# A decode step with cached attention: loops for the query and key products, one product for the maximum, x added by VectorE, the last values in four pieces, branch hints at the ends of two programs

## The chip, the cores and the metric

The kernel runs on one core of one Trainium2 chip. It is written for the engines directly, without a scheduler: TensorE (PE) multiplies, VectorE (DVE) does element work, reductions and transposes, ScalarE (ACT) exponentials and GELU, GpSimd (POOL) a few small passes, and SyncE (SP) issues nearly all DMA transfers. The metric is device time in microseconds (us), the median of three runs.

## The reference

One token passes through an attention block with a cache and then through an MLP block. All inputs are bfloat16.

```python
h  = x + A(layernorm(x))          # x: 1 x 1 x 512
h2 = h + B(layernorm(h))
# A: 32 query heads, 8 key heads, 16384 cached positions, head size 128
q = (x @ wq) ...                  # wq: 512 x 4096
scores = q . k * 128 ** -0.5
p = softmax(scores)
o = p . v
A = o @ wo                        # wo: 4096 x 512
# B, for one position: its shifted parts are all zeros, so x1 = x
h2 = gelu(layernorm(x1) @ w3) @ w4      # w3: 512 x 1792, w4: 1792 x 512
B = x1 + h2
```

Four query heads share a key head. With a sequence of length one the four shifted slices of the MLP's first stage hold only padding, so w1 and w2 do not enter the result, and the kernel never loads them. What it must read is wq (4 MB), keys and values (32 MB each), wo (4 MB), w3 and w4 (1.8 MB each).

## The kernel before

The work goes by pairs of key heads: four pairs, each with 8 MB of keys and 8 MB of values. Three big buffers in SBUF hold what is loaded: `kb[0]` and `kb[1]` (4 MB each, the two halves y = 0 and 1 of a pair's keys) and `vb` (8 MB, a pair's values). wq comes into `vb` first, wo into `kb[0]` and w3 and w4 into `kb[1]` at the end. SP issues the loads in program order, each when the last readers of its buffer are done: `load_keys(j + 1, y)` (L361) waits for the key transposes of half y, `load_values(j + 1)` (L370) for the value products of pair j. The keys of pair 1 come as one load of 8 MB, the other keys as two of 4 MB.

`Program` (L24) collects operations per engine with what they read and write, works out the semaphore waits and writes out each engine's program. SP, ACT, POOL and DVE get straight programs (`_run`, L128). TensorE's program has a loop over the pairs (`_tensor`, L136): block `pe_pair` with an inner block `pe_half` run twice (L206) and then `pe_rest` (L220); registers hold the semaphore values to wait for. Behind the loop stands a branch that is never taken, `pe_leave` (L236), which carries a branch hint marked at the start of the program (L191).

The stages:

- Start: x is loaded as 4 rows, spread over the partitions by a product with `quarter` (L463), and normalised on DVE (`row_sums` L392, `variance`, `seeds`, `inverse_root`), giving `xn`.
- Query product (L497 to L504): 32 products of 64 columns by 512, written out, four per half row of a PSUM bank; eight DVE transposes (L505) and four copies (L511) bring the query into `qb`.
- Per pair: DVE copies the pair's query to `qn` (L592). Per half: eight key transposes of 128x1024 words (L520), each followed on TensorE by four score products (L528) that add into one PSUM bank; the products are written out, 32 per half.
- `softmax` (L536): a maximum per row on DVE (L539), a product that turns it into a row (L540), a maximum per head on DVE (L542), a product that spreads it over the partitions (L544), the bias (L546), the exponential on ACT (L550), two transposes (L554).
- `values` (L557): 64 products of 32 columns by 512 (L562) when the whole 8 MB of values have landed.
- `gather` (L567): the sum of the exponentials by a product (L570), four DVE passes (L575, L578), a product (L581), the reciprocal (L583), the result into `o_m` (L584).
- Tail: 32 products with wo (L624), a product that adds x (L628), a copy (L631), four products (L633), the second normalisation, w3 (L645), GELU on ACT (L657), transposes (L661), w4 (L666), the last sum (L670) and the store (L672).

## Time and profile before

| what | us |
|---|---|
| median of 3 runs | 191.99 |
| lowest, highest | 191.99, 193.09 |
| profiled execution, its own time | 192.09 |
| its span, from the first to the last instruction | 190.8 |
| TensorE products busy | 109.7 |
| VectorE busy | 116.7 |
| ScalarE busy | 9.1 |
| GpSimd busy | 7.4 |

The span is taken by the hardware profiler inside the execution; 1.3 us of the execution's own time lie around it. The profile page gives busy times per engine, a row that shows the mean busy share of the 16 DMA engines in 40 equal slices, the DMA queues, and the chain of work that ended last. Lines of the timeline read: start, duration, engine, line, operation, output and inputs, and in brackets the idle time ahead of it and what ended it. Queue issues of SP are marked SPq. The clock that TensorE was granted was 0.82 in the mean, with stretches at 0.5. Memory reads come to 79.17 MB, at a mean of 415 GB/s over the span.

### The profile page before, as it was taken

The page shows a single profiled execution, that of the slowest core. Times are in us where ns is not written, and L with a number is a line of the kernel's source. Part 1 is how long each engine was busy: PE and PEld are TensorE (multiplying, and loading weights), DVE is VectorE, ACT ScalarE, POOL GpSimd, SP SyncE. Part 2 cuts the span into 40 slices and gives each one's busy share as a digit, 9 for nine tenths or more (in the row PEclk, how much of TensorE's full clock was granted, in tenths as well). Part 3 has the DMA queues.
Part 4 walks back from the last instruction along what each step waited for, and adds up shares of the span by engine and source line. Part 5 has one row for each costly group of instructions (what it writes and reads, how often), then busy time and mean ns, then how long its engine had stood idle before and what let it go on. Part 6 is the DMA issues. An engine that isn't in the chain of part 4 may idle for free.

```text
span 190.8 us, 1799 instructions
## 1 busy us (share of the span) xinstructions
PE 109.7 (58%) x694; PEld 41.3 (22%) x694; DVE 116.7 (61%) x184; ACT 9.1 (5%) x15; POOL 7.4 (4%) x16
## 2 busy tenths in 40 slices
PE   0128099892093006999256599934749896056543
PEld 0113034220031002432013133211313322022213
DVE  7746497984404009998443999935289995503372
ACT  3000000002000000000200000010000000500020
POOL 7100000000000000000000000000000000000041
PEclk9999958999559755899958879995797999558975
DMA  6999999999999999997999999979999899999990
GB/s 227 433 440 440 440 440 441 440 440 440 440 440 440 440 440 440 440 426 344 433 440 440 543 440 426 440 337 440 426 426 488 371 440 398 440 423 411 433 371 20
DMA packets 2612, 79.22 MB, mean 415 GB/s; under 512 B 304, under 2 KB 432, under 8 KB 560
## 3 DMA queue, kind: packets, MB, share of 16 engines
q1 hardware_dynamic: 2600, 79.17, 96.7%
q8 instruction: 2, 0.03, 0.1%
q14 instruction: 2, 0.02, 0.0%
q10 hardware_dynamic: 8, 0.00, 0.0%
HBM read 79.17 MB, written 0.00 MB: 415 GB/s over the span
## 4 chain that ended last, share of the span: by engine, by line
DMA 60%; DVE 32%; PE 5%; issue 1%; ACT 1%; SPq 1%; ACTq 0%
DMA kb<-in_A_k_cache_dram 45%; DVE kt L520 28%; DMA kb<-in_B_w_dram 15%; PE O_ps L562 3%; DVE pt L554 1%; PE mn_ps L666 1%; DVE mx L539 1%; ACT p_sb L550 1%; SPq L355 1%; DVE od L578 1%; PE s_ps L528 1%; PE A_ps L581 0%; PE mn_ps L544 0%; PE mn_ps L540 0%; DVE od L575 0%
## 5 line engine op out<-in xcount | busy, mean ns | idle before, releaser
L528 PE MATMUL s_ps<-kt,qn 128*128 128x512 bf16 x256 | 70.2, 417 | 26.0 <-DVE kt L520 23.9
L520 DVE STREAM_TRANSPOSE kt<-kb 128x1024 int32<-128x1024 int32 x64 | 72.8, 1208 | 15.0 <-DMA kb<-in_A_k_cache_dram 15.0
L528 PEld LDWEIGHTS s_ps<-kt,qn 128*128 128x128 bf16 x256 | 23.5, 104 | 71.9 <-issue 36.6
L562 PE MATMUL O_ps<-vb,pt 128*32 128x512 bf16 x256 | 22.6, 530 | 21.7 <-DMA vb<-in_A_v_cache_dram 13.5
L575 DVE TENSOR_SCALAR od<-O_ps,rowc 128x128 f32<-128x128 f32 x4 | 1.4, 350 | 28.3 <-PE mn_ps L570 28.3
L562 PEld LDWEIGHTS O_ps<-vb,pt 128*32 128x32 bf16 x256 | 8.5, 128 | 34.2 <-issue 23.9
L554 DVE STREAM_TRANSPOSE pt<-p_sb 64x1024 bf16<-64x1024 bf16 x8 | 9.9, 1239 | 5.4 <-ACT p_sb L550 5.3
L550 ACT ACTIVATE p_sb<-s_ps,bias 128x1024 bf16<-128x1024 f32 x4 | 4.5, 1114 | 156.0 <-DVE nmh L546 156.0
L539 DVE TENSOR_REDUCE mx<-s_ps 128x1 f32<-128x1024 f32 x4 | 4.9, 1224 | 4.6 <-PE s_ps L528 4.6
L438 POOL TENSOR_SCALAR st<-st 128x1 f32<-128x1 f32 x1 | 0.2, 242 | 177.4 <-DVE st L423 177.4
L501 PE MATMUL O_ps<-vb,xn 128*64 128x512 bf16 x16 | 3.3, 586 | 5.8 <-DMA vb<-in_A_wq_dram 5.8
L581 PE MATMUL A_ps<-od,zo 128*32 128x128 f32 x8 | 1.6, 285 | 6.4 <-DVE den L583 6.4
L540 PE MATMUL mn_ps<-ident_f,mx 128*1 128x128 f32 x8 | 1.5, 270 | 5.3 <-DVE mx L539 5.3
L578 DVE SCALAR_TENSOR_TENSOR od<-O_ps,rowc,od 128x128 f32<-128x128 f32 x12 | 4.2, 351 | 0.4
L460 DVE CAST ident<-ident_f 4x4 bf16<-4x4 f32 x1 | 3.8, 3849 | 0.6 <-POOL ident_f L455 0.6
L505 DVE STREAM_TRANSPOSE qcol<-O_ps 128x256 f32<-128x256 f32 x4 | 1.6, 428 | 4.0 <-PE O_ps L501 4.0
L463 PE MATMUL O_ps<-x,quarter 4*128 4x128 bf16 x1 | 0.3, 283 | 5.8 <-DVE quarter L461 5.8
L501 PEld LDWEIGHTS O_ps<-vb,xn 128*64 128x64 bf16 x16 | 1.5, 165 | 7.2 <-issue 7.2
L666 PE MATMUL mn_ps<-kb,hcol 128*32 128x128 bf16 x56 | 1.7, 309 | 2.0 <-DMA kb<-in_B_w_dram 2.0
L645 PE MATMUL s_ps<-kb,hc 128*32 128x448 bf16 x16 | 1.7, 572 | 1.4 <-DMA kb<-in_B_w_dram 1.4
L624 PE MATMUL O_ps<-kb,o_b 128*32 128x512 bf16 x32 | 1.9, 380 | 1.1 <-DVE o_b L620 1.1
L584 DVE SCALAR_TENSOR_TENSOR o_m<-A_ps,den,maskdd 32x128 f32<-32x128 f32 x4 | 1.4, 340 | 1.7 <-PE A_ps L581 1.7
(78 smaller groups left out, 45.0 us busy)
## 6 DMA issues: line engine op xcount, KB each, us to landing
kb<-in_A_k_cache_dram SPq DMA_DIRECT2D x6, 4096.0 KB, 23.2
vb<-in_A_wq_dram SPq DMA_DIRECT2D x1, 4096.0 KB, 12.4
kb<-in_A_wo_dram SPq DMA_DIRECT2D x1, 3072.0 KB, 27.0
kb<-in_B_w_dram SPq DMA_DIRECT2D x1, 1792.0 KB, 24.6
kb<-in_B_w_dram SPq DMA_DIRECT2D x1, 1280.0 KB, 27.9
kb<-in_A_wo_dram SPq DMA_DIRECT2D x1, 1024.0 KB, 29.1
kb<-in_B_w_dram SPq DMA_DIRECT2D x1, 384.0 KB, 28.4
kb<-in_B_w_dram SPq DMA_DIRECT2D x1, 128.0 KB, 28.2
```

The costliest lines, as they stand in the source:

```text
L355: P.op(by, lambda e: e.dma_start(dst, src), w=[key, *also], dma=name)
L460: dve(lambda e: e.tensor_copy(ident[:, :], ident_f[0:4, 0:4]), r=["ident_f"], w=["ident"])
L501: pe(lambda e, row=row, k=k, g=g, at=at: e.matmul(row[64 * g:64 * g + 64, :], copies(xn[:, k:k + 1], 64), wq_sb[:, at:at + REP * DH], star ...
L520: dve(lambda e, view=view: e.transpose(view(kt), view(kb[y])), r=[("r", y, n) for n in range(RPARTS)], w=[("kt", t)])
L528: pe(lambda e, n=n, c=c: e.matmul(s_ps[:, bass.ds(P.y, 1), :], qn[:, n, QPAD - 4 * c:QW - 4 * c], ktv[:, n // 2, n % 2, :, 8 * c:8 * c + 8 ...
L539: dve(lambda e: e.tensor_reduce(mx[:, :], s_all, AX.X, ALU.max), r=[("s", 0), ("s", 1)], w=["mx"], **both)
L550: act(lambda e: e.activation(p_sb[:, :], s_all, ACTF.Exp, bias=bias[:, 0:1], scale=float(SCALE), accum_out=acc[:, :]), r=[("s", 0), ("s", ...
L554: dve(lambda e, g=g: e.transpose(pt[64 * g:64 * g + 64, :, :, g, :], p_sb[64 * g:64 * g + 64, :]), r=["p"], w=["pt"])
L562: pe(lambda e, q=q, ct=ct, xl=xl, ch=ch: e.matmul(O_ps[0][32 * ct:32 * ct + 32, :], pt[:, xl, ch, :, :].rearrange("p g u -> p (g u)"), til ...
L578: dve(lambda e, block=block, c=c: e.scalar_tensor_tensor(od[:, :], block, rowc[:, c:c + 1], od[:, :], ALU.mult, ALU.add), r=[key, "rowc", ...
L624: pe(lambda e, r_=r_, q=q: e.matmul(O_ps[0][32 * q:32 * q + 32, :], copies(o_b[:, r_:r_ + 1], 32), wo_sb[:, r_ * D:(r_ + 1) * D], start=(r ...
L666: pe(lambda e, m=m, o=o: e.matmul(n_ps[32 * o:32 * o + 32, 0:128], hcol[:, m, :], w4_sb[:, m, o * 128:(o + 1) * 128], start=(m == 0), stop ...
```

## The change

- Query product: 32 products of the full 128 columns in a loop of eight rounds with four products each; each round writes a PSUM bank of its own, chosen by a register. Four transposes of 64 partitions by 1024 replace eight of 128 by 256.
- Key product: a loop of eight pieces per half with four products each; a register picks the slice of the query and of the transposed keys. A product with zeros now starts the bank ahead of the loop. The key transposes go two pieces at a time, except in the last half of the last pair; each adds as many to the semaphore as it holds pieces.
- Maximum: the row maxima are multiplied into a diagonal on DVE, and one product with the constant `mean4` (all entries -1 / (32 * 512)) gives every partition the negated row; DVE takes minima. The second product and its constant go.
- The sum of the exponentials and its reciprocal move ahead of the value products.
- Values: TensorE waits for a semaphore that GpSimd raises when a load has landed. The last pair's values are loaded in four pieces of 2 MB, and the value products go in four parts of 16.
- x: the spread x is kept in `hx`, and DVE adds it in the pass that also sums the row; the product at L628 goes.
- Programs: all work stands in a block named `body`; the programs of DVE and TensorE end with a branch that is never taken and carries a hint marked at their start, and the branch and hint behind the pair loop go.
- A helper `more` for extra products is added; nothing calls it.

```diff
...
+    def _vector(self):
+        eng = self.nc.vector
+        rv = eng.alloc_register("never")
+        hint = eng.mark_branch_hint_location()
+        eng.reg_mov(rv, 0)
+        self._run(eng, self.ops["DVE"], {})
+        eng.br_lt(rv, 0, "body", "pe_query").branch_hint(hint)
...
-        nc.switch_bb("pe_leave", parent=None)
-        eng.br_lt(rj, 0, "pe_pair", "pe_after").branch_hint(hint)
...
+        nc.switch_bb("pe_query", parent=None)
+        width = D
+        self.b = eng.snap(rk, min_val=0, max_val=2 * pairs - 1)
+        self.c = eng.snap(rq, min_val=0, max_val=width * (2 * pairs - 1))
+        for o in query:
+            self._issue(eng, o)
+        eng.reg_add(rk, rk, 1)
+        eng.reg_add(rq, rq, 2 * width)
+        eng.br_lt(rq, 2 * width * pairs, "pe_query", "pe_queried")
+        nc.switch_bb("pe_queried", parent=None)
+        self.b = self.c = None
+        eng.reg_add(rq, rq, width - 2 * width * pairs)
+        eng.br_lt(rq, 2 * width, "pe_query", "pe_pair")
...
+        for a in places("clear", 1, 0):
+            self._issue(eng, at[a])
+        eng.reg_mov(rq, QPAD)
+        eng.reg_mov(rk, 0)
+        eng.br("pe_piece")
+        nc.switch_bb("pe_piece", parent=None)
+        self.q = eng.snap(rq, min_val=0, max_val=QPAD)
+        self.k = eng.snap(rk, min_val=0, max_val=8 * (pieces - 1))
+        eng.reg_add(r, r, 1)
+        eng.wait_ge(vector, r)
+        for a in places("key", 1, 0, 1):
+            self._issue(eng, at[a])
+        eng.reg_add(rq, rq, -4)
+        eng.reg_add(rk, rk, 8)
+        eng.br_lt(rk, 8 * pieces, "pe_piece", "pe_halved")
...
+        straight("middle")
+        for x in range(parts):
+            eng.reg_add(rl, rl, 1)
+            eng.wait_ge(sem, rl)
+            for a in places("value", 1, x):
+                self._issue(eng, at[a])
+        straight("rest")
+        eng.reg_add(r, r, first - (final - step))
+        eng.br_lt(rl, v0 - 1 + parts * pairs, "pe_pair", "pe_after")
...
+        eng.br_lt(rl, 0, "pe_pair", "pe_end").branch_hint(hint)
+        nc.switch_bb("pe_end", parent=None)
...
-            load("v", vb[:, :], pair_rows(A_v_cache, j), "v")
+            n = 64 * DH
+            if j < PAIRS - 1:
+                load("v", vb[:, :], pair_rows(A_v_cache, j), ("v", 0),
+                     also=[("v", x) for x in range(1, 4)] + [("landed", x) for x in range(4)])
+                P.op("POOL", lambda e: e.nop(), r=[("v", 0)], w=[("landed", x) for x in range(4)], worth=4,
+                     own="v")
+                return
+            for x in range(4):
+                load(f"v{x}", vb[:, x * n:(x + 1) * n], pair_rows(A_v_cache, j)[:, x * n:(x + 1) * n], ("v", x),
+                     also=[("landed", x)])
+            for x in range(4):
+                P.op("POOL", lambda e: e.nop(), r=[("v", x)], w=[("landed", x)], own="v")
...
-            dve(lambda e: e.tensor_scalar(hr[:, :], row[:, 0:128], 0.0, 0.0, ALU.add, ALU.add,
-                                          accum_out=rs[i][:, 0:1]), r=[key], w=["hr", ("rs", i, 0)], bank=[key])
+            h, hk = (hr, "hr") if i else (hx, "hx")
+            if i:
+                dve(lambda e: e.scalar_tensor_tensor(h[:, :], row[:, 0:128], 1.0, hx[:, :], ALU.mult, ALU.add,
+                                                     accum_out=rs[i][:, 0:1]),
+                    r=[key, "hx"], w=[hk, ("rs", i, 0)], bank=[key])
...
-        rows = [(O_ps[0][:, :], ("O", 0)), (O_ps[1][:, :], ("O", 1)), (s_ps[:, 0, :], ("s", 0)), (s_ps[:, 1, :], ("s", 1))]
-        for j, (row, key) in enumerate(rows):
+        keys = [("s", 0), ("s", 1), ("O", 0), ("O", 1), "A", "mn", "spare0", "spare1"]
+        wq_k = wq_sb[:, 0:NCH * HQ * DH].rearrange("p (k c) -> p k c", k=NCH)
+        for i, key in enumerate(keys):
+            P.part("query", i)
             for k in range(NCH):
-                for g in range(2):
-                    at = k * HQ * DH + (2 * j + g) * REP * DH
-                    pe(lambda e, row=row, k=k, g=g, at=at: e.matmul(
-                        row[64 * g:64 * g + 64, :], copies(xn[:, k:k + 1], 64), wq_sb[:, at:at + REP * DH],
-                        start=(k == 0), stop=(k == NCH - 1)), r=["xn", "v"], w=[key], bank=[key])
+                pe(lambda e, k=k: e.matmul(banks[:, bass.ds(P.b, 1), :], copies(xn[:, k:k + 1], 128),
+                                           wq_k[:, k, bass.ds(P.c, REP * DH)], start=(k == 0), stop=(k == NCH - 1)),
+                   r=["xn"] + [("v", x) for x in range(4)], w=["n" if key == "mn" else key], bank=[key])
+        P.part()
+        for g in range(2):
+            row = banks[64 * g:64 * g + 64, PAIRS * g:PAIRS * g + PAIRS, :].rearrange("p j c -> p (j c)")
             for b in range(2):
-                dve(lambda e, j=j, b=b, row=row: e.transpose(
-                    qcol[:, j, 2 * REP * b:2 * REP * (b + 1), :].rearrange("p m u -> p (m u)"),
-                    row.rearrange("p (h b i e) -> p b e h i", b=2, i=32, e=2)[:, b, :, :, :]),
-                    r=[key], w=["qcol"], bank=[key])
+                dve(lambda e, g=g, b=b, row=row: e.transpose(
+                    qcol[64 * g:64 * g + 64, 2 * b:2 * b + 2, :, :].rearrange("p e m u -> p (e m u)"),
+                    row.rearrange("p (m b i e) -> p b e m i", b=2, i=32, e=2)[:, b, :, :, :]),
+                    r=["n" if x == "mn" else x for x in keys[PAIRS * g:PAIRS * g + PAIRS]], w=["qcol"],
+                    bank=keys[PAIRS * g:PAIRS * g + PAIRS])
...
-        def transpose_keys(y, ts):
-            for t in ts:
+        def transpose_keys(y, n):
+            for t in range(0, 8, n):
                 view = lambda x, t=t: x[:, :].bitcast(I32).rearrange("p (x l w) -> p x (l w)", x=2, l=64)[
-                    :, :, t * 512:(t + 1) * 512]
-                dve(lambda e, view=view: e.transpose(view(kt), view(kb[y])),
-                    r=[("r", y, n) for n in range(RPARTS)], w=[("kt", t)])
+                    :, :, t * 512:(t + n) * 512]
+                P.op("DVE", lambda e, view=view: e.transpose(view(kt), view(kb[y])),
+                     r=[("r", y, i) for i in range(RPARTS)], w=[("kt", t + i) for i in range(n)], worth=n)
         ktv = kt[:, :].rearrange("p (x l b s e) -> p b e x l s", x=2, l=64, b=2, s=32, e=2)
-        def scores(j, y, cs):
-            for c in cs:
+        none = qn[:, 0, 0:1]
+        def scores(j, y):
+            P.part("clear", j, y)
+            pe(lambda e: e.matmul(s_ps[:, bass.ds(P.y, 1), :], copies(none, 128), copies(none, 512),
+                                  start=True, stop=False, skip_group_check=True),
+               r=["qn"], w=[("s", y)], bank=[("s", y)])
+            for c in range(8):
+                P.part("key", j, y, c)
                 for n in range(4):
-                    pe(lambda e, n=n, c=c: e.matmul(
-                        s_ps[:, bass.ds(P.y, 1), :], qn[:, n, QPAD - 4 * c:QW - 4 * c],
-                        ktv[:, n // 2, n % 2, :, 8 * c:8 * c + 8, :],
-                        start=(c == 0 and n == 0), stop=(c == 7 and n == 3)),
+                    pe(lambda e, n=n: e.matmul(
+                        s_ps[:, bass.ds(P.y, 1), :], qn[:, n, bass.ds(P.q, 128)],
+                        ktv[:, n // 2, n % 2, :, bass.ds(P.k, 8), :],
+                        start=False, stop=(n == 3), skip_group_check=True),
                        r=["qn", ("kt", c)], w=[("s", y)], bank=[("s", y)])
...
-            pe(lambda e: e.matmul(m_ps[0:1, 0:128], mx[:, :], ident_f[:, :], start=True, stop=True),
-               r=["mx", "ident_f"], w=["m"], bank=["mn"])
-            dve(lambda e: e.tensor_reduce(nm[:, :, :], m_ps[0:1, 0:128].rearrange("o (g n h) -> o g h n", g=2, h=REP),
-                                          AX.X, ALU.max), r=["m"], w=["nm"], bank=["mn"])
-            pe(lambda e: e.matmul(n_ps[:, 0:2 * REP], nscale[0:1, :], nm[:, :, :].rearrange("o g h -> o (g h)"),
-                                  start=True, stop=True), r=["nm", "nscale"], w=["n"], bank=["mn"])
-            dve(lambda e: e.scalar_tensor_tensor(nmh[:, :], n_ps[:, 0:2 * REP], 1.0,
-                                                 maskgh[:, :, :].rearrange("p g h -> p (g h)"), ALU.mult, ALU.mult,
-                                                 accum_out=bias[:, :]), r=["n", "maskgh"], w=["nmh", "bias"],
-                bank=["mn"])
+            dve(lambda e: e.tensor_scalar(mxd[:, :], ident_f[:, :], mx[:, 0:1], None, ALU.mult),
+                r=["mx", "ident_f"], w=["mxd"])
+            pe(lambda e: e.matmul(m_ps[:, 0:128], mean4[:, :], mxd[:, :], start=True, stop=True),
+               r=["mxd", "mean4"], w=["m"], bank=["mn"])
+            dve(lambda e: e.tensor_reduce(nm[:, :, :], m_ps[:, 0:128].rearrange("p (g n h) -> p g h n", g=2, h=REP),
+                                          AX.X, ALU.min), r=["m"], w=["nm"], bank=["mn"])
+            dve(lambda e: e.scalar_tensor_tensor(nmh[:, :], nm[:, :, :].rearrange("p g h -> p (g h)"),
+                                                 32 * D * SCALE, maskgh[:, :, :].rearrange("p g h -> p (g h)"),
+                                                 ALU.mult, ALU.mult, accum_out=bias[:, :]),
+                r=["nm", "maskgh"], w=["nmh", "bias"])
...
         def values(j):
             tiles = vb[:, :].rearrange("p (x c l d) -> p x l c d", x=4, c=8, l=8)
-            for q in range(16):
-                for ct in range(4):
-                    xl, ch = 2 * q + ct // 2, ct % 2
-                    pe(lambda e, q=q, ct=ct, xl=xl, ch=ch: e.matmul(
-                        O_ps[0][32 * ct:32 * ct + 32, :], pt[:, xl, ch, :, :].rearrange("p g u -> p (g u)"),
-                        tiles[:, xl // 8, xl % 8, 4 * ch:4 * ch + 4, :], start=(q == 0), stop=(q == 15)),
-                       r=["v", "pt"], w=[("O", 0)], bank=[("O", 0)])
+            for x in range(4):
+                P.part("value", j, x)
+                for it in range(4):
+                    for ct in range(4):
+                        l, ch = 2 * it + ct // 2, ct % 2
+                        pe(lambda e, x=x, l=l, ct=ct, ch=ch: e.matmul(
+                            O_ps[0][32 * ct:32 * ct + 32, :], pt[:, 8 * x + l, ch, :, :].rearrange("p g u -> p (g u)"),
+                            tiles[:, x, l, 4 * ch:4 * ch + 4, :], start=(x == 0 and l < 2), stop=(x == 3 and l >= 6)),
+                           r=[("landed", x), "pt"], w=[("O", 0)], bank=[("O", 0)])
+        def sums(j):
+            pe(lambda e: e.matmul(n_ps[0:32, 32:33], zd[:, :], acc[:, :], start=True, stop=True),
+               r=["acc", "zd", "pt"], w=["n"], bank=["mn"])
+            dve(lambda e: e.reciprocal(den[:, :], n_ps[0:32, 32:33]), r=["n"], w=["den"], bank=["mn"])
         def gather(j):
...
-                transpose_keys(y, range(8))
-                scores(j, y, range(8))
+                transpose_keys(y, 1 if j == PAIRS - 1 and y else 2)
+                scores(j, y)
                 if j < PAIRS - 1:
                     load_keys(j + 1, y)
+            P.part("middle", j)
+            softmax(j)
+            sums(j)
+            values(j)
...
-        pe(lambda e: e.matmul(h_ps[:, 0:128], quarter[:, :, :].rearrange("p q u -> p (q u)"), x4[:, :],
-                              start=True, stop=False, skip_group_check=True),
-           r=["quarter", "x4"], w=[hkey], bank=[hkey])
         dve(lambda e: e.tensor_copy(osum[:, :], O_ps[0][:, :]), r=[("O", 0)], w=["osum"], bank=[("O", 0)])
         for q in range(4):
             pe(lambda e, q=q: e.matmul(h_ps[32 * q:32 * q + 32, 0:128], copies(row32[:, 0:1], 32),
-                                       osum[:, q * 128:(q + 1) * 128], start=False, stop=True, skip_group_check=True),
+                                       osum[:, q * 128:(q + 1) * 128], start=True, stop=True),
...
```

## The prediction, made before the changed kernel was run

> **What bounds the kernel now.** I read the page first: the share of the DMA engines, the queues and the chain that ended last.

> ```profile
> span 190.8 us, 1799 instructions
> ...
> DMA  6999999999999999997999999979999899999990
> ...
> q1 hardware_dynamic: 2600, 79.17, 96.7%
> q8 instruction: 2, 0.03, 0.1%
> q14 instruction: 2, 0.02, 0.0%
> ...
> DMA 60%; DVE 32%; PE 5%; issue 1%; ACT 1%; SPq 1%; ACTq 0%
> ```

> The reader sees one queue, q1, that keeps sixteen DMA engines busy for 96.7% of the span. The 32% of DVE in the chain mislead: the chain steps to DVE because a transpose released the issue of a load, but the load then stood in a full queue. The timeline of SP, the issuing engine, shows how early each load was issued:

> ```profile
> 18.40 0.33 SPq L355 DMA_DIRECT2D vb<-in_A_v_cache_dram  x1
> 42.41 0.33 SPq L355 DMA_DIRECT2D kb<-in_A_k_cache_dram  x1
> 58.55 0.33 SPq L355 DMA_DIRECT2D vb<-in_A_v_cache_dram  x1
> 81.09 9.29 SPq L355 DMA_DIRECT2D kb<-in_A_k_cache_dram  x2
> 103.26 0.33 SPq L355 DMA_DIRECT2D vb<-in_A_v_cache_dram  x1
> 115.04 9.34 SPq L355 DMA_DIRECT2D kb<-in_A_k_cache_dram  x2
> 137.30 0.33 SPq L355 DMA_DIRECT2D vb<-in_A_v_cache_dram  x1
> ```

> The trace's packet records give when the transfer ahead of each landed (sixteen 4-byte marks per transfer, one from each DMA engine; the last one counts): 32.14, 52.04, 71.39, 90.74 (and 100.45 for the second of the two issues), 110.18, 129.53 (139.25), 148.96. So the issues were early by 13.7, 9.6, 12.8, 9.6, 6.9, 14.5 and 11.7 us. An issue needs about 1.0 us (first issue 0.72, first packet 1.74). The queue never ran dry, and the tightest place is the third values, with 6.9 - 1.0 = 5.9 us. Whatever happens ahead of an issue is free up to that sum.

> The tail is the one place where time can move. Its timeline:

> ```profile
> 182.20 0.40 ACT L639 ACTIVATE hc<-hT,st 128x128 bf16<-128x128 f32 x1 [17.03 <-DVE st L404]
> ...
> 183.42 1.69 PE L645 MATMUL s_ps<-kb,hc 128*32 128x448 bf16 x16 [1.45 <-DMA kb<-in_B_w_dram]
> ...
> 185.15 0.85 ACT L657 ACTIVATE hg<-s_ps,st 128x224 bf16<-128x224 f32 x2 [2.55 <-PE s_ps L645]
> 185.67 1.04 DVE L661 STREAM_TRANSPOSE hcol<-hg 128x224 bf16<-128x224 bf16 x2 [0.83 <-ACT hg L657]
> ...
> 187.06 1.71 PE L666 MATMUL mn_ps<-kb,hcol 128*32 128x128 bf16 x56 [1.96 <-DMA kb<-in_B_w_dram]
> 188.80 0.29 DVE L670 TENSOR_TENSOR fin<-xsum,mn_ps 128x128 bf16<-128x128 f32 x1 [2.09 <-PE mn_ps L666]
> 189.12 0.63 SPq L672 DMA_DIRECT2D out_dram<-fin  x1
> ```

> Both product groups start 0.6 us after the last mark of their load: w3's at 182.81, the first part of w4's at 186.46. Those last marks are late by themselves: of w3's sixteen, fourteen are in by 181.80, the others at 182.40 and 182.81. The records say why. Four packets of the run are instructions, not data (the q8 and q14 lines above). One of 8 KB at 31.75 stretches a data packet on its engine to 3.042 us (median 2.420), and in every transfer from there on one engine ends 0.6 us behind the fifteenth (52.04 against 51.46; still 178.10 against 177.50). One of 16 KB at 180.24 stretches a packet of w3 to 1.039 (median 0.537), one at 184.72 a packet of w4 to 1.044 (0.387). The fourth, at 188.42, follows the data.

> **The change, part by part.**
> *Loops and fewer instructions.* By the order of instructions, TensorE's program shrinks from about 542 to 438 (a product counts as a weight load and a product, a float32 one twice that); DVE's from about 196 trace records to 180 (28 key transposes fewer, some others added). The two fetches put down to DVE come at its records 56 and 192, so 180 do not reach the second. TensorE fetched nothing while its pair loop ran (its hint stood right behind that loop), and the two q8 packets come after the loop ended at 176.33. With the hints at the ends of both programs I take it that no fetch falls into the data. That is the one term that counts. Bounds: all four stay as they are (0), or the three go.

> *The sum of the tail.* w3's last mark goes from 182.81 to 181.80, -1.01. The last values in 4 pieces make packets of 16 KB: between 14336 bytes at 0.537 and 24576 at 0.912 that is 0.612 each, four 2.448 against 2.420, over 8 per engine +0.22, and three more marks +0.03: +0.25. So w3's products start at 183.42 - 0.76 = 182.66; hc ends at 182.60 now and no later after, so it doesn't hold them. From there GELU and its transposes take 3.29 to 186.71, but GELU also needs the inverse root, now done at 184.84 (0.31 before GELU). hc and the root move up with the output product: the last values land in four pieces, 48 of 64 products are done before the last piece, the gather comes about 2 us earlier, but the wo products then wait for wo's own load (marks to 178.10), which leaves 0.3 to 0.8. I take -0.65 for hcol: 186.06. The first part of w4 is in on the undisturbed engines at 184.88, + 0.25 + 0.6 = 185.7, so hcol now decides: products at 186.1 instead of 187.06, -0.95. The 1.71 of products, fin and the store stay. The profiled execution took 192.09 (span 190.8 and 1.3 around it), 0.1 above the median 191.99: 192.09 - 0.95 = **191.1**.

> *Query product as a loop.* 32 full-width products against 32 of 64 columns, two of which ran side by side (16 in 3.31 us, then 16 in 1.91). Full-width rows of L528 give 0.427 and 0.213 us at half and full clock; from 13.27 at half until about 16.5, then full: 7 x 0.427 + 25 x 0.213 = 8.3 us, to 21.6 against 18.31; branches of 0.22 (below) lie beside running products. Four transposes of 64x1024 follow, two behind the products: the page has 1.24 for 64x1024 from SBUF. With the copies the first key transpose moves from 22.84 to about 26, the second half from 33.23 to about 35. First values: 13.7 of cover; keys 1: 9.6. Cost 0.

> *Key product as a loop.* Not shown by the page's busy rows, but the trace has records of such instructions in the old loops: a fused register operation 41 to 52 ns (2 or 3 steps), a compare-and-branch 79 not taken and 220 to 245 taken. A piece has seven fused operations of 2 to 6 steps; at 5 ns a step more, 0.37 us, and 0.22 for the branch, 0.1 to dispatch: 0.7 against 1.14 of a key transpose (9.13 for 8). Bounds: 0.6, and 1.3 if six steps cost twice three's. Even 1.3 adds 16 x 0.16 = 2.6 us to a pair, below 5.9. A clearing product adds 0.2 to 0.4 per half. Cost 0. Transposes in twos: between equal and 0.07 saved each; the last two pieces' eight products then trail by 1.7 instead of 0.9. In the last half the pieces are single.

> *Maximum in one product.* Out: one product with its two hops (161.76 to 162.18, 0.42); in: one DVE pass over 128x128 float32 (L398: 0.29). -0.1 per pair on a covered chain, 0. The denominator moves ahead of the values: 0.3 to 0.5 us of TensorE, covered. x on VectorE: replaces a product that ran at 179.54 beside osum; the DVE pass keeps its 0.29. 0. GpSimd passes the values' landing on: one hop, 0.05 to 0.2; in the last pair wo's load covers it.

> [...]

> **Rivals.**
> - *The fetches stay, or come elsewhere in the data* (0.2). For it: no row shows a hint on DVE at work. Then only the 16 KB pieces are left: 192.09 + 0.25 = 192.3 (191.8 to 192.8).
> - *Slower: the key loop becomes TensorE's bound* (0.12), by a fetch at its back branches or by address operations far dearer than their shorter kin. It decides from 5.9 / 16 = 0.37 us per piece above the transposes' 1.14, that is 1.51. At 2.0 a pair's chain grows by 16 x 0.86 = 13.8, the third values are 7.9 late, the next pair adds some 6: about 206; at 1.7, 9.0 - 5.9 = 3 and about as much again: 198. Against it: 0.22 per taken branch and no instruction packet from 31.75 to 180.24 in eight passes of the old half loop.
> - *The tail also runs at full clock* (0.1). L666 took 1.71 at a granted 0.5; the clock windows move with TensorE's work. Then 0.5 to 0.8 less: 190.4.

> **How the numbers follow.** My forecast has 0.58, with 190.6 to 191.8 as its own range. The range 190.2 to 192.9 takes in the first and third rivals and leaves out the slower one. A measurement here can tell about 1% (1.9 us) from no change. Faster by over 1% means below 190.1: a piece of the third rival, 0.06. Slower by over 1%, above 193.9: 0.12. Within 1%: 0.82.

> **What would show it.** Right: the q8 and q14 instruction lines of the queues vanish or fall behind the data; w3's products start near 182.7, w4's near 186.1; DMA still in nines throughout; the values' issues still earlier than the transfer ahead lands. Wrong: instruction packets inside the span, key products spaced over 1.5 us a piece, a slice of the DMA row below 7 in the middle, or an issue after the queue drained.

## The result, and the profile after

The changed kernel takes 200.61 us (median of 4 runs, 199.21 to 201.18). Against the kernel before on the same chip its ratio is 1.0426, with an interval of 1.0369 to 1.0483: it is slower, and 200.61 lies far outside the range of 190.2 to 192.9. The profiled execution took 199.21, 7.12 more than the one of before.

These are rows of the changed kernel's profile page, the same ones as were shown of before:

```profile
span 196.6 us, 2321 instructions
...
DMA  6999999999999999998999999999999999999800
...
q1 hardware_dynamic: 3032, 79.17, 94.0%
q14 instruction: 1, 0.01, 0.0%
...
DVE 35%; PE 33%; DMA 20%; issue 8%; ACT 2%; ACTq 0%; DVEq 0%; SPq 0%
```

Two things are to be seen. The DMA row holds its nines (one 8 among them) until the loads are done, and its last two slices are empty: the loads are no later than before, and something else ends last. The chain of waits says what: DMA falls from 60% to 20%, PE rises from 5% to 33%. And one instruction packet is left inside the span, where there were four. I read an instruction packet as an engine fetching its program and call it a fetch below. Those of 16 KB stand on queue q8, those of 8 KB on q14; they are put down to TensorE and to VectorE, because the times of the former change with TensorE's hint and those of the latter with VectorE's in the runs below. SP's timeline confirms the loads:

```profile
61.18 0.33 SPq L430 DMA_DIRECT2D vb<-in_A_v_cache_dram  x1
...
105.80 0.33 SPq L430 DMA_DIRECT2D vb<-in_A_v_cache_dram  x1
...
139.73 3.59 SPq L430 DMA_DIRECT2D vb<-in_A_v_cache_dram  x4
...
193.89 0.63 SPq L780 DMA_DIRECT2D out_dram<-fin  x1
```

The transfer ahead of the third values lands at 109.58 by the packet records, so their issue at 105.80 is early by 3.8 us (6.9 before). The queue never ran dry, and the last data land at 186.51, 1.3 us sooner than before (187.78). The tail comes later all the same:

```profile
183.40 1.91 PE L735 MATMUL banks<-kb,o_b 128*32 128x512 bf16 x32 [1.06 <-DVE o_b L731]
187.91 0.40 ACT L747 ACTIVATE hc<-hT,st 128x128 bf16<-128x128 f32 x1 [14.13 <-DVE st L500]
188.36 1.35 PE L753 MATMUL banks<-kb,hc 128*32 128x448 bf16 x16 [0.69 <-ACT hc L747]
191.21 1.05 DVE L769 STREAM_TRANSPOSE hcol<-hg 128x224 bf16<-128x224 bf16 x2 [0.62 <-ACT hg L765]
191.84 1.69 PE L774 MATMUL banks<-kb,hcol 128*32 128x128 bf16 x56 [2.12 <-DVE hcol L769]
193.58 0.29 DVE L778 TENSOR_TENSOR fin<-xsum,banks 128x128 bf16<-128x128 f32 x1 [1.32 <-PE banks L774]
```

The products with wo, w3 and w4 wait for o_b (the attention output), hc (the input of w3) and hcol (the transposed GELU output), for results; before, w3's and w4's waited for their loads. The last sum comes at 193.58 instead of 188.80: 4.78 of the 7.12. The rest lies behind it. From the store's issue to the end of the span it takes 2.66 instead of 1.67: by the packet records an instruction packet of 8 KB starts at 195.04, and one of the store's four packets starts behind it (195.60; the others at 195.12 to 195.15). That one lands at 196.52, the others by 195.52; before, all four landed by 190.75, 1.63 behind the issue. And 2.66 us of the execution lie around the span instead of 1.31; instruction packets of 8 KB at 197.60 and of 16 KB at 198.48 fall there. 4.78 + 1.00 + 1.35 is the 7.12 but for rounding.

Where the 4.78 come from can be added up from the stages (a key stage is counted from the first key transpose of a pair to its row maximum, DVE's pass over the scores):

| us | before | after |
|---|---|---|
| pair 0: first key transpose | 22.84 | 26.51 |
| pair 1: first key transpose | 71.89 | 71.34 |
| key stage of pairs 0, 1, 2, 3 | 20.65, 19.28, 19.28, 19.85 | 22.79, 22.83, 22.74, 22.72 |
| row maximum to gather, pairs 1, 2 | 12.05, 12.14 | 11.58, 11.89 |
| last exponentials transposed | 166.18 | 174.79 |
| last values: products start | 168.91 | 174.93 |
| w3 products start | 183.42 | 188.36 |
| w4 products start | 187.06 | 191.84 |
| last sum | 188.80 | 193.58 |

Pair 0 is covered by the wait for the second pair's keys: pair 1 starts even earlier. From there nothing resets the chain: -0.55 + 3.55 + 3.46 + 2.87 - 0.47 - 0.25 = 8.61, which is 174.79 - 166.18. Then the slack of the tail is used up. Before, the last value products waited for their load, 2.73 behind the transposed exponentials; after, they follow them by 0.15:

```profile
168.91 5.71 PE L562 MATMUL O_ps<-vb,pt 128*32 128x512 bf16 x64 [6.76 <-DMA vb<-in_A_v_cache_dram]
```

```profile
174.93 5.38 PE L669 MATMUL banks<-vb,pt 128*32 128x512 bf16 x64
```

Between the end of hc and w3's products 0.82 becomes 0.05. These two waits take 3.35 out of the 8.61; the work between them is 0.31 shorter, and the stretch from w3's products to w4's 0.16. That leaves the 4.78.

What a pair does in its 3.5 us more is seen in the weight loads of the key products, four per piece, and in the key transposes beside them. Before, in pair 2:

```profile
119.52 0.55 PEld L528 LDWEIGHTS s_ps<-kt,qn 128*128 128x128 bf16 x4 [0.57 <-DVE kt L520]
120.65 0.55 PEld L528 LDWEIGHTS s_ps<-kt,qn 128*128 128x128 bf16 x4 [0.57 <-DVE kt L520]
```

and after:

```profile
117.18 8.85 DVE L619 STREAM_TRANSPOSE kt<-kb 128x2048 int32<-128x2048 int32 x4
...
121.44 0.58 PEld L633 LDWEIGHTS banks<-kt,qn 128*128 x4 [0.44 <-issue]
...
122.66 0.56 PEld L633 LDWEIGHTS banks<-kt,qn 128*128 x4 [0.64 <-issue]
...
126.34 0.61 PEld L633 LDWEIGHTS banks<-kt,qn 128*128 x4 [0.64 <-issue]
...
127.59 0.56 PEld L633 LDWEIGHTS banks<-kt,qn 128*128 x4 [0.64 <-issue]
```

Before, a piece took 1.13 and the idle time ended with a transpose (kt). After, it takes 1.19 to 1.25 and the idle time ends with "issue": no tensor is waited for, while the transposes make two pieces in 2.21 (8.85 for eight). VectorE is through so early that it waits 5.09 for the products ahead of the row maximum, instead of 1.14.

In pair 2 the 3.46 add up from the starts of these weight loads: 1.20 for the first piece, 0.82 and 0.78 for the seven steps from piece to piece within each half, and 0.67 for the step from the first half to the second (1.88 instead of 1.21), where the clearing product and the branch of the half loop stand (their shares are not separated).

The profile page does not count register instructions, which TensorE's sequencer runs, as busy; the trace's records of one piece show what fills the gap (start in us, length in ns, the sequencer's instruction):

```
121.439   95 LDWEIGHTS        121.468  74 FUSED_REGOPS
121.592   96 LDWEIGHTS        121.621  74 FUSED_REGOPS
121.744   96 LDWEIGHTS        121.804  74 FUSED_REGOPS
121.928   96 LDWEIGHTS        121.957  42 FUSED_REGOPS
122.057  216 COMPARE_BRANCH   122.331  47 FUSED_REGOPS
122.436   74 FUSED_REGOPS     122.568  42 FUSED_REGOPS
122.659   96 LDWEIGHTS (the next piece)
```

The four weight loads are 0.15 to 0.18 apart, 0.49 in all, and from the last one to the next piece it takes 0.73: four register operations and the branch are 0.42 of it, and 0.31 is time between them: 58 ns from one's end to the next one's start, 49 from the last one's end to the next weight load. 0.49 + 0.73 = 1.22.

My theory (theory 1): the instruction stream of the key loop paces the products; the transposes in twos let the first piece start 2.58 us behind the first transpose instead of 1.38; the chain of pairs 1, 2, 3 and the tail has slack for only part of it; and the hints (BRANCH_PREFETCH_HINT in the trace, at the marked place: 0.74 on VectorE, 0.80 on TensorE) put instruction fetches at the end, where nothing covers them. Rivals: the loss comes from the transposes in twos alone, from the other parts (the maximum, the values in pieces, the clearing product), or from the fetches alone.

### The profile page after: what moved, and what is told of

It reads as the page before. It is cut to its first block, busy times and chain, and to the rows that moved or that the text cites. A ratio compares the mean times of both kernels' runs of the same rounds, so it can differ in the third digit from the quotient of the medians.

```text
span 196.6 us, 2321 instructions
## 1 busy us (share of the span) xinstructions
PE 114.1 (58%) x693; PEld 44.4 (23%) x693; DVE 118.0 (60%) x155; ACT 9.0 (5%) x15; POOL 7.3 (4%) x16
## 3 DMA queue, kind: packets, MB, share of 16 engines
q1 hardware_dynamic: 3032, 79.17, 94.0%
HBM read 79.17 MB, written 0.00 MB: 403 GB/s over the span
## 4 chain that ended last, share of the span: by engine, by line
DVE 35%; PE 33%; DMA 20%; issue 8%; ACT 2%; ACTq 0%; DVEq 0%; SPq 0%
DVE kt L619 21%; PE banks L633 17%; DMA kb<-in_A_k_cache_dram 14%; PE banks L669 8%; DMA vb<-in_A_wq_dram 6%; PE banks L596 5%; DVE pt L659 4%; DVE mx L644 2%; ACT p_sb L655 2%; DVE od L688 2%; PE banks L735 1%; PE banks L774 1%; PE banks L647 1%; DVE qcol L603 1%; PE banks L691 1%
## 5 line engine op out<-in xcount | busy, mean ns | idle before, releaser
L633 PE MATMUL banks<-kt,qn 128*128 x256 | 70.5, 411 | 23.1 <-DVE kt L619 16.9
L619 DVE STREAM_TRANSPOSE kt<-kb 128x2048 int32<-128x2048 int32 (+1 forms) x36 | 70.9, 2037 | 7.6 <-DMA kb<-in_A_k_cache_dram 7.6
L633 PEld LDWEIGHTS banks<-kt,qn 128*128 x256 | 26.1, 102 | 66.1 <-issue 52.8
L669 PE MATMUL banks<-vb,pt 128*32 128x512 bf16 x256 | 20.7, 495 | 0.0
L644 DVE TENSOR_REDUCE mx<-banks 128x1 f32<-128x1024 f32 x4 | 4.9, 1224 | 20.2 <-PE banks L633 20.2
L685 DVE TENSOR_SCALAR od<-banks,rowc 128x128 f32<-128x128 f32 x4 | 1.4, 350 | 19.5 <-PE banks L669 19.5
L596 PE MATMUL banks<-vb,xn 128*128 x32 | 9.2, 461 | 6.1 <-DMA vb<-in_A_wq_dram 6.1
L655 ACT ACTIVATE p_sb<-banks,bias 128x1024 bf16<-128x1024 f32 x4 | 4.5, 1114 | 164.6 <-DVE nmh L651 164.6
L669 PEld LDWEIGHTS banks<-vb,pt 128*32 128x32 bf16 x256 | 8.1, 121 | 10.7 <-issue 7.6
L603 DVE STREAM_TRANSPOSE qcol<-banks 64x1024 f32<-64x1024 f32 x4 | 4.8, 1228 | 8.6 <-PE banks L596 8.6
L688 DVE SCALAR_TENSOR_TENSOR od<-banks,rowc,od 128x128 f32<-128x128 f32 x12 | 4.2, 351 | 0.4
```

Source lines behind the costliest of these rows:

```text
L596: pe(lambda e, k=k: e.matmul(banks[:, bass.ds(P.b, 1), :], copies(xn[:, k:k + 1], 128), wq_k[:, k, bass.ds(P.c, REP * DH)], start=(k == 0) ...
L603: dve(lambda e, g=g, b=b, row=row: e.transpose(qcol[64 * g:64 * g + 64, 2 * b:2 * b + 2, :, :].rearrange("p e m u -> p (e m u)"), row.rear ...
L619: P.op("DVE", lambda e, view=view: e.transpose(view(kt), view(kb[y])), r=[("r", y, i) for i in range(RPARTS)], w=[("kt", t + i) for i in r ...
L633: pe(lambda e, n=n: e.matmul(s_ps[:, bass.ds(P.y, 1), :], qn[:, n, bass.ds(P.q, 128)], ktv[:, n // 2, n % 2, :, bass.ds(P.k, 8), :], start ...
L644: dve(lambda e: e.tensor_reduce(mx[:, :], s_all, AX.X, ALU.max), r=[("s", 0), ("s", 1)], w=["mx"], **both)
L655: act(lambda e: e.activation(p_sb[:, :], s_all, ACTF.Exp, bias=bias[:, 0:1], scale=float(SCALE), accum_out=acc[:, :]), r=[("s", 0), ("s", ...
```

## The experiments

All are the changed kernel with an edit; the first four ran beside the kernel before at 192.14, the next four at 192.15, then at 192.20 and 192.31.

**Key products written out** ("unroll"): the loop over pieces goes, and the addresses stand in the instructions again. The clearing product and the transposes in twos stay.

```diff
-        eng.br("pe_piece")
-        nc.switch_bb("pe_piece", parent=None)
...
-        eng.br_lt(rk, 8 * pieces, "pe_piece", "pe_halved")
+        for c in range(pieces):
+            eng.reg_add(r, r, 1)
+            eng.wait_ge(vector, r)
+            for a in places("key", 1, 0, c):
+                self._issue(eng, at[a])
...
```

> The changed kernel with the key product written out again (32 products per half, addresses in the instructions, one register addition and wait per piece; the clearing product and the transposes in twos stay). Theory 1, the register operations and the branch of the eight-piece loop pace TensorE's instruction stream at 1.24 us a piece against 1.13 of a transpose: from the first key transpose of a pair to the row maximum 19.5 to 19.9 us in place of 22.7, three such pairs in a chain, so the last value products end early enough that the loads bound the tail again; what the hints cost at the end stays: 193.5 to 194.5. Rival, the transposes in twos make TensorE late: 22 us a pair stays and 199 to 200. Rival, only the fetches at the program's end count: 199 to 200.

194.2 us, ratio 1.010 (1.0069 to 1.0131). The key stages fall to 19.04 to 19.67, the last sum to 188.62; 6.4 of the 8.6 us are gone. The groups of weight loads show the pace change hands; after:

```profile
L633 PEld LDWEIGHTS banks<-kt,qn 128*128 x256 | 26.1, 102 | 66.1 <-issue 52.8
```

and with the products written out:

```profile
L622 PEld LDWEIGHTS banks<-kt,qn 128*128 128x128 bf16 x256 | 25.3, 103 | 60.0 <-DVE kt L608 26.7 <-issue 10.8
```

Idle time ended by "issue" falls from 52.8 to 10.8, and the largest part that the view names now ends with a transpose. TensorE can also catch up again: in the second half of pair 1 most pieces follow one another by 0.87, where the loop's take 1.19 to 1.25.

**Two pieces per round** ("two"): four rounds of eight products, half the branches and fewer register operations.

```diff
-        eng.reg_add(r, r, 1)
+        eng.reg_add(r, r, 2)
...
-        for a in places("key", 1, 0, 1):
-            self._issue(eng, at[a])
+        for c in range(2):
+            for a in places("key", 1, 0, c):
+                self._issue(eng, at[a])
...
```

> The changed kernel with the key loop in four rounds of two pieces (eight products a round, half the branches, one wait per two pieces). Theory 1: per round 0.13 and 0.09 for the first address operations, eight times 0.157, and 0.55 for the counters and the branch, about 2.1 us, that is 1.05 a piece and so under the transposes' 1.13: from the first transpose to the maximum 19.6 to 20.2 us, total 193.5 to 195. If the address operations alone set the pace and not the branch: more than 2.3 a round, 21 to 22 us a pair, 197 to 199.

194.1, ratio 1.0097 (1.0066 to 1.0128), key stages 19.87 to 20.12. So register addresses and a loop cost nothing here by themselves; what cost was the loop's fixed part per four products, the 0.73 from the last weight load to the next piece. With two pieces per round it is as fast as without a loop (194.1 and 194.2).

**Transposes one piece at a time** ("single"): `transpose_keys(y, 1)` everywhere, the loop stays.

> The changed kernel with all key transposes one piece at a time, the eight-piece loop kept. Theory 1: only the first piece comes 1.1 us earlier, the pace of 1.24 stays: 21.5 to 21.8 us from the first transpose to the maximum, and 196 to 198 in all. Rival, the twos are the cause: 19.3 us a pair as before, 193 to 195.

199.13, ratio 1.0328 (1.0266 to 1.0391). The key stages fall by 1.0, to 21.72 to 21.75, as theory 1 has it: about a third of the 3.46 is the later first piece. So the rival that blames the twos for all of it falls. The total missed my expectation, though. The profiled execution is even slower than that of the changed kernel, although no fetch falls at its end (the only one is of 8 KB, at 34.17): from the store's issue to the end of the span it takes 1.68 again, but the last sum comes at 196.54, 2.96 later. After, and then with single transposes:

```profile
core 0: 196.6 us, clock 0.850
```

```profile
core 0: 198.5 us, clock 0.801
```

The stretches at half clock are longer (three of 10.2 us instead of 6.8) and fall on the value products: from the row maximum to the gather it takes 13.13 and 13.16 in pairs 1 and 2 instead of 11.58 and 11.89, and from the last gather to the last sum 14.70 instead of 13.20. The four runs go with the clock: 200.1 and 199.97 at 0.801, 198.3 at 0.808, 197.69 at 0.825. I read from these rows that the granted clock is part of the time here, where TensorE's chain is the bound; no run changes the clock alone, so neither this nor its share is shown. The changed kernel's own four runs do not follow it that strictly (199.21 at 0.850, 200.29 at 0.851, 200.93 at 0.835, 201.18 at 0.827).

**Hints as before** ("nohint"): none on VectorE, TensorE's right behind the pair loop.

```diff
-        hint = eng.mark_branch_hint_location()
...
-        eng.br_lt(rv, 0, "body", "pe_query").branch_hint(hint)
...
+        nc.switch_bb("pe_leave", parent=None)
+        eng.br_lt(rl, 0, "pe_pair", "pe_after").branch_hint(hint)
...
-        eng.br_lt(rl, 0, "pe_pair", "pe_end").branch_hint(hint)
...
```

> The changed kernel with the hints as before: none on DVE, TensorE's behind the pair loop. The chain of the pairs stays (22.7 us a pair, the last sum at about 193.6 to 193.9). If the hints moved the fetches to the end, where one delays the store by 1.0 us and two lie behind it for 1.3: total 2.3 us less, 197.5 to 199, with instruction packets inside the data again. If the hints are harmless: 200 to 201.

198.95, ratio 1.0356 (1.0318 to 1.0394). Key stages 22.77 to 22.80, unchanged; store to span end 1.68, around the span 1.3, both as in the kernel before. So the fetches are not the main loss; the hints cost 1.7 us. That is a net figure: the profiled execution's end is 2.3 shorter, but its last sum comes at 195.29, not near 193.6 as I expected. Fetches are in its data again (at 55.98 and 187.16), pair 1 starts 0.7 later and the values take longer; the runs do not separate these.

**Both undone** ("unroll_nohint").

> The changed kernel with its key products written out (32 per half, as before the change) and the branch hints as they were before (none on VectorE, TensorE's right behind the pair loop). Theory 1 (the register instructions pace the key products, and the chain of pairs 1 to 3 and the tail has no slack for it; the rest of the loss is an instruction fetch at the end of the programs, ahead of the store): row maximum 19.0 to 19.9 us behind the first key transpose, store to span end 1.7, own time less span 1.3; a fetch of 8 KB or 16 KB falls into the data again; total 192.0 to 192.6, level with the kernel before. Rival (the hints cost nothing, what is left of the loss lies in the single product for the maximum, the values in pieces or the clearing products): as with the hints at the ends, 193.5 to 194.5.

191.99, ratio 0.9986 (0.9965 to 1.0007): level with before. With the three runs above this is a complete table: loop and hints 200.61, loop alone 198.95, hints alone 194.2, neither 191.99. The loop costs 6.4 to 7.0, the hints 1.7 to 2.2, and all that remains (one product for the maximum, x on VectorE, values in pieces, the query loop, the clearing products, the transposes in twos) is together worth nothing that can be measured once the key products are written out. The rival of the other parts falls. The fetches are back in the data, by the packet records: 16 KB at 179.31, on an engine that then ends w3's transfer last, at 183.00 (181.81 in a run below without a fetch there).

**Hinted branches moved forward**, ahead of the w4 products on TensorE and of the GELU transposes on VectorE, with the two-piece loop, with the products written out, and with the loop as it is.

```diff
-        self._run(eng, self.ops["DVE"], {})
+        self.have = {}
+        self._run(eng, self.ops["DVE"][:-3], self.have)
         eng.br_lt(rv, 0, "body", "pe_query").branch_hint(hint)
...
-        for o in ops[hi:]:
+        for o in ops[hi:-56]:
...
+        self._run(eng, ops[-56:], seen)
+        self._run(nc.vector, self.ops["DVE"][-3:], self.have)
```

> The changed kernel with two pieces per round of the key loop (4 rounds of 8 products) and the two hinted branches moved from the ends of the programs to the place ahead of the w4 products (TensorE) and of the GELU transposes (VectorE). Theory 1: the pace of the key products is that of the transposes, row maximum 19.8 to 20.1 behind the first key transpose; if the fetch comes where the branch stands, it falls behind the data and ahead of the end: last data 186.5, store to span end 1.7, own less span 1.3, total 190.3 to 191.5, below both kernels. If the place of the branch does not set the time of the fetch: a fetch at 60 in the data and one or two at the end again, 194.

> The changed kernel with its key products written out and the two hinted branches moved ahead of the w4 products (TensorE) and of the GELU transposes (VectorE). Theory 1 with fetches that follow the branch: row maximum 19.0 to 19.9 behind the first key transpose, last data 186.5 to 187.6, total 190.5 to 192. If the place of the branch does not set the time of the fetch: fetches at the end again, 194.2 as with the hints at the ends.

> The changed kernel with nothing but the two hinted branches moved ahead of the w4 products (TensorE) and of the GELU transposes (VectorE); the key loop keeps eight rounds of one piece. Theory 1: the chain stays (row maximum 22.7 to 22.8 behind the first key transpose, last sum at 193.6), and the end gets shorter by the fetches that stand ahead of the store and behind it: store to span end 1.7, own less span 1.3, total 197 to 198. Rival (the loss is all at the end, the chain is covered): 192. If the place of the branch does not matter: 200 to 201.

193.82 (1.0072, 1.0046 to 1.0098), 193.67 (1.0071, 1.0045 to 1.0097) and 201.43 (1.0459, 1.0415 to 1.0504). The gain that I expected did not come in any of the three, though with the products written out both its conditions did: the last data land at 186.22, w3's last mark comes at 181.81, and behind the store the end is as short as before (1.67 and 1.3). VectorE's timeline of that run shows why:

```profile
184.53 0.17 DVE L531 SCALAR_TENSOR_TENSOR st<-st,sti 128x1 f32<-128x1 f32 x1
188.04 1.05 DVE L761 STREAM_TRANSPOSE hcol<-hg 128x224 bf16<-128x224 bf16 x2 [3.35 <-issue]
190.42 0.29 DVE L770 TENSOR_TENSOR fin<-xsum,banks 128x128 bf16<-128x128 f32 x1 [1.33 <-PE banks L766]
```

GELU is done at 185.6, but VectorE stands still from 184.70 to 188.04, right behind its hinted branch, and a fetch of 8 KB starts at 186.19 in that time. The other two runs have the same standstill, of 3.40 and 3.38. What was exposed at the end is now exposed 3 us earlier.

**One hint at a time**, with the products written out: VectorE's at the end and TensorE's behind the pair loop; TensorE's at the end and none on VectorE; TensorE's ahead of the w4 products and none on VectorE. The edits are those above, for one engine each.

> The changed kernel with its key products written out, VectorE's hinted branch at the end of its program as in the change, TensorE's right behind the pair loop as before the change. Theory 1 as the run with both branches moved forward sharpens it (VectorE stood still for 3.35 us ahead of the instruction behind its hinted branch): the branch that is never taken has its engine fetch the code that follows, about 3.3 us, which lies bare where nothing covers it. VectorE ends at 188.8, its fetch then ends near 192, behind the store's landing near 190.5: total 193.3 to 194.3, as with both hints. Rival (it is TensorE's branch that costs): 192.0 to 192.4.

> The changed kernel with its key products written out, TensorE's hinted branch at the end of its program as in the change, none on VectorE. Theory 1: TensorE ends 0.4 us ahead of VectorE, so its fetch of about 3.3 us ends 1 to 1.5 us behind what ends the program now: total 192.3 to 193.5. Rival (it is VectorE's branch alone that costs): 191.8 to 192.2.

> The changed kernel with its key products written out, TensorE's hinted branch moved ahead of the w4 products, none on VectorE. Theory 1: TensorE's fetch lies in its wait for the GELU transposes and behind most of the data, so the end has no bare fetch and w3's last mark comes at 182.0 to 182.4 instead of 183.0: last sum at 187.5 to 188.0, total 190.7 to 191.5, a little below both kernels. Rival (the fetch holds TensorE beyond the transposes, as it held VectorE): w4's products start at 187.3 or later, total 191.8 to 193.5.

193.71 (1.0074, 1.0048 to 1.0100), 192.08 (0.9979, 0.9958 to 1.0001) and 194.35 (1.0089, 1.0058 to 1.0120). VectorE's hint at the end costs all of the 1.7, with fetches of 8 KB at 190.44 and 192.90. TensorE's at the end costs nothing: here my expectation missed and its rival held; its fetch of 16 KB at 189.89 runs beside the store and ends 0.15 behind the span. TensorE's moved forward costs 2.3, more than my expectation and its rival allowed, again by a standstill:

```profile
186.27 1.15 PE L760 MATMUL banks<-kb,hcol 128*32 128x128 bf16 x35 [1.44 <-DMA kb<-in_B_w_dram]
190.05 0.82 PE L760 MATMUL banks<-kb,hcol 128*32 128x128 bf16 x21 [2.64 <-issue]
```

This time it is not behind the branch but 35 products further, and a 16 KB packet starts with it, at 187.40.

**VectorE's hinted branch between pair 0 and pair 1** ("unroll_dve_cover"), where it waits 11 us for keys.

> The changed kernel with its key products written out, TensorE's hinted branch at its end, and VectorE's hinted branch moved to the place between pair 0 and pair 1, where VectorE waits some 10 us for the second pair's keys. Theory 1 (a hinted branch that is not taken only puts the engine's next fetch off until it is needed; it costs about 3 us of that engine, and time only where nothing covers it): VectorE fetches near 60, behind the branch and ahead of 71, the end has neither the 1.6 us nor a late store; total 191.8 to 192.4, level with TensorE's hint alone at the end (192.08). Rival (a hint on VectorE costs time wherever its branch stands): 193.5 to 194.3.

193.65 (1.0066, 1.0041 to 1.0091). The expectation missed and its rival held: VectorE has no fetch near 60 (the 16 KB at 58.62 are TensorE's) and none before 190.36 and 192.97, and the end is as exposed as with the branch there. So the place of the branch does not by itself set the time of the fetch. One thing is regular. In the four variants of the changed kernel without a hint on VectorE, its first fetch comes at 53.25 to 55.98, under the loads. With the hint, wherever its branch stands, it comes at 186 or later in all runs but one: in "single", where VectorE has 64 key transposes instead of 36, it came at 34.17. What sets the time stays open. What is shown is the price: 1.6 to 2.5 us in the runs where an engine's fetch came late and uncovered (2.5 is the loop as it is with the branches forward, 201.43 against 198.95). No kernel tried beats the one before beyond its interval.

## Why the prediction was wrong

**The step that failed** is the key loop: "Even 1.3 adds 16 x 0.16 = 2.6 us to a pair, below 5.9. ... Cost 0." It failed twice.

*Its size.* A piece took 1.19 to 1.25, not 0.7. The instructions themselves were priced well: the seven register operations are 0.43 (0.37 forecast) and the branch 0.22 (as forecast; in the changed kernel TensorE's records have 215 to 248 ns where it is taken and 76 to 79 where it is not). What I left out is the 58 ns between one and the next, and the places that the weight loads take in the same stream: together 0.58, where I had 0.1 to dispatch, a term that no run shows. The piece still lay within the bounds of 0.6 to 1.3; the pair's growth, 3.46 in pair 2, did not stay under 2.6, because two terms were missing from it. The twos cost 1.20 at the first piece of a pair, where I had priced only the last pieces, and the step between the halves cost 0.67.

*What it was held against.* 5.9 was the slack of the third values' issue, and that slack held: the issue came 3.8 early. But a delay that no issue feels isn't gone. Pairs 1, 2 and 3 and the tail are one chain, and its slack is what the tail waited for its loads, 3.35, or 3.8 with what the tail itself became shorter (8.61 less the 4.78 that are left), once, and not 5.9 in each pair. Three times 3.3 had to pass through it. For the same reason the rival of a slower key loop, which has happened, was given a deciding point of 1.51 us per piece and a chance of 0.12; it decides from little above the transposes' own 1.11. Even my upper bound, put in the right place, gives 3 x 2.6 = 7.8 less 3.8, 4 us slower: the prediction had the number that was needed.

**The fetches.** "With the hints at the ends of both programs I take it that no fetch falls into the data" was right for the changed kernel, and so was its effect: w3's last mark came at 182.10 (forecast 182.05, before 182.81). It is no rule: with the same hints, the runs "unroll" and "two" have a fetch of 16 KB in the data, at 58.28 and 60.61. The part of the -0.95 up to w3's products existed: where the products were written out and the branches moved forward, these products started at 182.52 (forecast 182.66, before 183.42). In no run here did it reach the end of the program, where fetches stood ahead of the store or ahead of an instruction. I never asked what a fetch that leaves the data is late for.

What a fetch cost differed from run to run. TensorE's at 189.89 cost nothing (192.08 against 191.99), VectorE's at the end 1.7 us (193.71 against 191.99). Behind the 16 KB in the data at 179.31 w3's last mark comes at 183.00 instead of 181.81. The fetch at the back branches that the slower rival names is not what slowed the loops: no instruction packet lies between 1 and 195 us of the changed kernel, and no branch took over 0.25.

**Right:** the query loop (first key transpose at 26.51, forecast about 26, covered by pair 1's keys; its products took 9.24 instead of 8.3), the values' pieces, x on VectorE, GpSimd's hop (together nothing, by the run with loop and hints undone). **Level, for another reason:** the one product for the maximum. From the maximum to the exponential it takes 2.72 before and after, so not even -0.1 was there: the diagonal pass and a longer product cost what a product less saves.

## What to carry to other kernels

Before a stage's growth is called covered, follow it to the end of the program: slack at a transfer's issue is not slack of the result, and where stages run one behind another without a wait that resets them, a small growth counts once per stage against a slack that exists only once (here 3.55, 3.46 and 2.87 against 3.8). A register loop is priced by its instruction stream from start to start, gaps included (here 1.19 to 1.25 a piece), against the pace of the engine that feeds it (1.11); two pieces per round were enough here to hide it (194.1, written out 194.2). When a fetch is gone from the data, look for it at the end, ahead of the store (here 8 KB at 195.04).
